# Retention attention and an ELU feed-forward on one core: half of the attention re-cut into chunks of 64 neighbouring tokens, with a new opening

## The chip, the cores and the metric

The kernel runs on one core of a Trainium2 chip. A core has TensorE (PE: matrix products; PEld is its loading of weights), VectorE (DVE), ScalarE (ACT), GpSimd (POOL) and SyncE (SP), which here only issues transfers; 16 DMA engines move data between the chip's main memory and the core's working memory SBUF. Matrix products land in PSUM, from which VectorE and ScalarE read. The metric is the device time of one execution in microseconds (us), lower is better, given as the median of several runs.

## What is computed

```
q, k, v: 8 batches x 8 heads x 576 tokens x 64, f32
scores = (q @ k^T) / 8
ret    = scores * gamma_h^(i-j) for i >= j, else 0      (gamma_h = 1 - 2^(-5-h))
x      = (ret @ v), heads side by side                  -> 4608 x 512
h      = x @ w_in                                       (512 x 2048)
g      = where(h > 0, h, exp(min(h, 0)) - 1)
out    = g @ w_out                                      (2048 x 512) -> 4608 x 512 f32
```

The decay gamma^(i-j) is split into a factor for the query row and one for the key row, so that both can be scaled ahead. Inside a chunk of tokens the masked scores are formed; what earlier chunks contribute goes through a running 64x64 sum of k^T v per head, the state.

## The kernel before

**Items.** A main item is one batch `b`, half `T` (tokens 0 to 255 or 256 to 511) and half `w` of the heads (four heads): 8 x 2 x 2 = 32 items, numbered 0 to 31 in batch order. The last 64 tokens of all batches make two tail items, four batches each. An item's tile of q, k or v has 128 partitions, and partition p holds the two neighbouring tokens 2p and 2p+1 of its 256 (`"h (p e) d -> p h (e d)"`, L375), so a piece read from main memory is 512 bytes. With `C = 64` partitions per chunk, a chunk is 128 tokens, two per item.

**Steps of an item.** Three loads on SyncE's queue (L375); q and k times their factors, four operations (L445, `cq`, `ck`), to bf16; v cast to bf16 (L479, `cv`); a transpose of q and k, for the first seven items on TensorE with copies back (L491, L497), from item 7 on by a DMA transpose on SyncE's queue (L530, `tr`). TensorE then makes scores (`do_scores`), state times queries (`do_inter`), values (`do_values`) and the new k^T v (`do_state`). VectorE multiplies the scores by the mask (L731, 1024 elements a partition). After the item's first chunk the running sum is `mid`, after its second `end` (L678 to L687); each is spread into a block-diagonal 128x128 tile, `s_mid` and `s_end` (L695, on GpSimd, or L709 for the first items). The result is copied into `xt` (L766), the input of the first layer.

**Stretches.** From the fifth item on, TensorE does one item's state times queries and values together with the next item's scores and k^T v, in one stretch (`stretch`). The first ones (`early`) come apart.

**Feed-forward.** Each block of 512 tokens (256 for the first three batches) goes through the first layer (`ffn1`: four matmuls, an exponential on ScalarE, then two VectorE operations, or one and one on ScalarE) and the second (`ffn2`), and out by SyncE. The weights come by GpSimd's queue in four pieces each (`wi0` to `wi3`, `wo0` to `wo3`).

**Order.** Nothing is ordered by hand: `Plan.run` plays the program through with a cost for each operation, transfers sharing the wire, a limit on buffers (`SLOTS`) and ranks, in which attention stands ahead of feed-forward by `LEAD`. What it picks is each engine's fixed program order. Constants named here: `HOP`, the time until another engine sees a result; `FROM`, when weight loads may be issued; `ON`, operations nailed to an engine; `AWAY`, a load put on ScalarE's queue (the first v). Where the plan leaves TensorE idle before 50 us, matmuls on zeros are put in.

Of the kernel before, what the change touches and what calls it, by code (L numbers as in the profile page):

```python
# [13 lines left out]
I32 = mybir.dt.int32  # L14
# [4 lines left out]
HOP = {"PE": 0.22, "DVE": 0.08, "ACT": 0.08, "POOL": 0.1}  # L19
# [3 lines left out]
class Op:  # L23


    def __init__(self, name, cost, deps, emit, rank, take=(), use=(), banks=(), dma=None, after=None):
        self.name, self.cost, self.emit, self.rank = name, cost, emit, rank
        self.deps = [d for d in deps if d is not None]
        self.turn = [] if after is None else [after]
        self.take, self.use, self.banks, self.dma = take, [*use, *(t[1] for t in take)], banks, dma  # L30
        self.eng = self.start = self.end = self.done = None
        self.slot, self.waits, self.at = {}, [], 0.0


class Plan:
# [6 lines left out]
    def add(self, *a, **kw):  # L42
        op = Op(*a, **kw)
        self.ops.append(op)
        for key in op.use:
            self.users.setdefault(key, []).append(op)
            op.turn += self.owner.get(key, [])
        for cls, key, *_ in op.take:
            self.owner[key] = [op]
            if cls not in FREE:  # L50
                op.turn += self.takers.get(cls, [])
                self.takers[cls] = [op]
        return op
# [12 lines left out]
    def run(self, began):  # L66

        self.left = {key: len(u) for key, u in self.users.items()}
        self.freed = {}
        bank, lanes = {}, {"SP": 0, "POOL": 0, "ACT": 0}  # L70
# [53 lines left out]
        while len(order) < len(self.ops) or any(wire.values()) or events:  # L124
            again = True
            while again:
                again = False
                for e in began:
# [9 lines left out]
                    op.eng, op.start, op.end = e, now, now + (cost[0] if isinstance(cost, tuple) else cost)  # L138
# [61 lines left out]
FROM = (8.9, 9.7, 10.5, 13.3, 16.6, 17.4, 18.2, 19.6)  # L200
ON = {}
DIRECT = True
AWAY = {("v", 0): 2.25}
# [7 lines left out]
FREE = ("f", "e", "em", "g", "ot")  # L211

# [4 lines left out]
    "xt": 3, "g": 28, "e": 4, "em": 4, "ot": 5, "mid": 4, "end": 4, "s_mid": 4, "s_end": 18,  # L217
# [4 lines left out]
def kernel(  # L222
# [56 lines left out]
    first = const.tile([P, 1], FP32, name="first")  # L279
    pin(nc.scalar.activation(first, zero[:, :1], AF.Exp))  # L280
# [13 lines left out]
    gk = const.tile([P, FT, H], FP32, name="gk")  # L294

# [58 lines left out]
    for n, it in enumerate(items):  # L354
        it.n = n
        it.early = n < FT
        it.xt = xt_of(it.blk)
        it.rank = n * 4 - 64 if it.early else base[it.blk] - LEAD + (
            16 * it.t if it.tail else 6 * it.w + (SPREAD * it.T if width[it.blk] > TB else 0))
# [3 lines left out]
    def load_main(it, srcs="qkv"):  # L363
# [3 lines left out]
        for s in srcs:  # L367
# [4 lines left out]

            def emit(op, src=src, key=key, away=away):
                dst = tiles[key].rearrange("p h e d -> p h (e d)")
                pin((nc.scalar if away else nc.sync).dma_start(  # L375
                    dst,
                    src[it.b, 4 * it.w : 4 * it.w + 4, 2 * P * it.T : 2 * P * (it.T + 1), :].rearrange(
                        "h (p e) d -> p h (e d)", e=2),
                ))

            take, use, held = [T(cls, key, [P, 4, 2, D], FP32)], [], []
            if s == "q" and n in HOLD:
                def emit_hold(op, key=key):
                    pin(nc.gpsimd.memset(tiles[key][:, 0, 0, :1], 0.0))

                held.append(add(f"hold{n}", {"POOL": 0.1}, [], emit_hold, -5, take=take))
                holds.append((held[0], HOLD[n]))
                take, use = [], [key]
            it.ld[s] = add(f"ld{s}{n}", {"ACT": 0.5} if away else {"SP": 0.46}, held, emit,
                           -10 ** 6 if away else len(plan.ops), take=take, use=use,  # L390
                           dma=(0.9, 32), after=None if away else chain.get(0))
# [28 lines left out]
    def load_w_in(n0, n1, after):  # L420
        c = slice(n0 * 512, n1 * 512)

        def emit(op):
            pin(nc.gpsimd.dma_start(w_in_sb[:, :, c], moe_w_in[:, c].rearrange("(j p) n -> p j n", p=P)))

        op = add(f"wi{n0}", {"POOL": 0.8}, [], emit, -1000, dma=(2.75 * (n1 - n0), 32 * (n1 - n0), 4.9), after=after)
        for n in range(n0, n1):
            w_in_ld[n] = op

    def load_w_out(n, after):  # L430
# [4 lines left out]
        w_out_ld[n] = add(f"wo{n}", {"POOL": 0.8}, [], emit, -1000, dma=(2.75, 32, 4.9), after=after)  # L435
# [3 lines left out]
    def scaled(it, i, e, cost):  # L439
        n = it.n  # L440
        key, raw = ("qkn", n), ("rq" + "qk"[i], n)
        g = (gq, gk)[i][:, 2 * it.T + e, 4 * it.w : 4 * it.w + 4].unsqueeze(2).to_broadcast([P, 4, D])
# [7 lines left out]
        op = add(f"c{'qk'[i]}{e}{n}", cost, [it.ld["qk"[i]]], emit, it.rank,  # L450
# [24 lines left out]
    def cast_v(it, cost):  # L475
        n = it.n

        def emit(op):
            pin(copy[op.eng](tiles["vn", n], tiles["rv", n]))  # L479

        it.cv = add(f"cv{n}", cost, [it.ld["v"]], emit, it.rank, take=[T("vn", ("vn", n), [P, 4, 2, D], BF16)],
                    use=[("rv", n)])

    def turn_pe(it, i, deps, src, key, dst_cls, n_of, cost):
# [8 lines left out]
        t = add(f"T{n_of}", {"PE": 0.35}, deps, emit, it.rank - 4,  # L493
# [12 lines left out]
    def prepare(it, turn):  # L506
# [21 lines left out]
        else:  # L528
            def emit(op):
# [3 lines left out]
                                 take=[T("qkT", ("qkT", n), [P, 8, P], BF16)], use=[("qkn", n)], dma=(1.7, 64)))  # L533
# [51 lines left out]

    def do_scores(it):
# [13 lines left out]
        tt = tiles["qkT", n]  # L600
        for hl in range(2):
# [9 lines left out]
    def do_inter(it, xkey):  # L611
        n = it.n
        if it.tail:
            for m in range(2):
                for j in range(2):
                    for hp in range(HP):
# [3 lines left out]
                            tiles["qkTt", n, m, j][:, hp, :ST])  # L620
            return
# [9 lines left out]
    def do_values(it, xkey):  # L631
# [12 lines left out]
        vn, pt = tiles["vn", n], tiles["pt", n]  # L644
        for hl in range(2):
# [7 lines left out]
    def do_state(it, views):  # L653
        n = it.n
        kn, vn = tiles["qkn", n], tiles["vn", n]
        for hl in range(2):
            for e in range(2):
                for c in range(2):
                    cs = slice(c * C, (c + 1) * C)
                    key, bank, ap = views[c]  # L660
                    for i in range(2):
                        acc(key, bank, i, ap()[i * D : (i + 1) * D, hl * D : (hl + 1) * D], kn[cs, 1, e, 2 * hl + i],
# [4 lines left out]
    def after_state(it, st, views, bank_keys):  # L667

        n = it.n
        prev = total.get(it.w) if it.T else None  # L670

# [48 lines left out]

    def mask_step(it, sc):
        n = it.n
        def emit(op):
            if it.tail:
# [5 lines left out]
                return  # L730
            pin(nc.vector.tensor_tensor(  # L731
# [5 lines left out]
        it.mask = add(f"mask{n}", {"DVE": 1.22}, [sc], emit, it.rank + 1,  # L737
                      take=[T("pt", ("pt", n), [P, 2, 2, 2 * P], BF16)], use=[("sc", n)], banks=[("sc", 0)])

    def inter_deps(it):  # L740
        if it.tail:
            return [*it.cvs, *(at[4 * it.t + j, 1, w].be for j in range(4) for w in range(2))]
        return [it.cv, it.bm] + ([at[it.b, 0, it.w].be] if it.T else [])

    def inter_uses(it):
# [3 lines left out]
        return [("s_mid", it.b, it.T, it.w), ("qkT", it.n), ("vn", it.n), ("pt", it.n)] + (  # L749
# [4 lines left out]
    def put_x(it, xkey, dep):  # L754

        for c in range(2):
            def emit(op, c=c):
# [4 lines left out]
                else:  # L762
                    src = xs[:, : 2 * P].rearrange("p (h e r) -> p h e r", h=2, e=2)
                    o = it.T * TB + c * P
                    dst = xt[:, 2 * it.w : 2 * it.w + 2, o : o + P].rearrange("p h (r e) -> p h e r", e=2)
                    pin(copy[op.eng](dst, src))  # L766
# [8 lines left out]
    def cost_of(it, parts):  # L775
        t = 0.0
        if "i" in parts:
# [18 lines left out]
    def stretch(prev, it):  # L796
# [12 lines left out]
        views = [((xkey, c), 0, lambda c=c: tiles[xkey, c][:, 2 * P : 3 * P]) for c in range(2)]  # L809
# [20 lines left out]
    def early(it):  # L830
        n = it.n
        sc = add(f"sc{n}", {"PE": 0.4}, it.turned, lambda op: do_scores(it), it.rank,
# [4 lines left out]
        st = add(f"st{n}", {"PE": 0.3}, [it.cq[1, 0], it.cq[1, 1], it.cv], lambda op: do_state(it, views), it.rank + 1,  # L837
# [112 lines left out]

    for it in items:
# [20 lines left out]
    def emit_factors(op):  # L972
        pin(nc.scalar.activation(gq[:, :FT], expo[:, :FT], AF.Exp, bias=bq))
        pin(nc.scalar.activation(gq[:, FT], expo[:, FT], AF.Exp, bias=bt))
        pin(nc.scalar.activation(gk, expo[:, :FT], AF.Exp, bias=bk, scale=-1.0))
# [36 lines left out]

    named = {op.name: op for op in plan.ops}
# [11 lines left out]
    order = plan.run({"PE": 1.3, "DVE": 2.2, "ACT": 2.25, "POOL": POOL0, "SP": 0.8})  # L1025
# [54 lines left out]
```

## Time and profile before

| | |
|---|---|
| median of 3 runs | 306.41 us (306.09 to 307.36) |
| the profiled execution | 306.02 us, of which the span shown is 303.8 us |
| busy: PE, DVE, ACT, POOL | 294.5, 210.1, 158.6, 148.3 us |
| granted TensorE clock | 1.0 throughout |
| main memory read, written | 36.70 MB, 9.44 MB |
| DMA packets under 512 B | 45841 of 103991 |

The span is the time from the first to the last instruction of the profiled execution. In a group's line stand: line of the program, engine, operation, tile written <- tiles read, size, count | busy time in us and mean ns of one | idle time of the engine before them, and what ended it. The row of 40 digits cuts the span into equal slices, each digit a busy share in tenths. The chain is the work that ended last, followed back from the end. Rows of the timeline give start, length, engine, line, operation and count. Rows of SPq, ACTq and POOLq are the issuing of transfers.

### The profile page before, as it was taken

To read this page: it belongs to the slowest core of one execution; us is meant where nothing else is said; L and a number is where in the kernel's file an instruction comes from. 1 tells how busy PE (TensorE), PEld (TensorE's weight loads), DVE (VectorE), ACT (ScalarE), POOL (GpSimd) and SP (SyncE) were. 2 spreads that over 40 slices of the span, in tenths; PEclk is the share of its full clock that TensorE was granted. 3 is DMA by queue.
4 is the path that set the end of the run, shared out by engine and by line. 5 is a ranking of instruction groups with operands and counts; after the bars stand their busy time and mean duration, and the time that the engine had idled before them with its cause. 6 is when DMAs were issued, how large, how long until landed. Compare 5 with 4: busy or idle time off the path is not lost.

```text
span 303.8 us, 8244 instructions
## 1 busy us (share of the span) xinstructions
PE 294.5 (97%) x3281; PEld 171.0 (56%) x3323; DVE 210.1 (69%) x380; ACT 158.6 (52%) x309; POOL 148.3 (49%) x252
## 2 busy tenths in 40 slices
PE   7899999999999999999999999999999999999996
PEld 3688656758767775554554444555554444444445
DVE  3978935749888888788787666768766666666600
ACT  4548724738765554687653434466544343444311
POOL 5980389987999998988886324322000000000000
PEclk9999999999999999999999999999999999999999
DMA  7999999999999999999997767311111111011132
GB/s 213 266 206 211 233 294 325 224 305 267 222 278 210 257 202 306 249 240 243 232 252 188 173 154 159 79 37 37 37 33 38 36 36 35 35 37 36 35 103 72
DMA packets 103991, 50.08 MB, mean 165 GB/s; under 512 B 45841, under 2 KB 99473, under 8 KB 103953
## 3 DMA queue, kind: packets, MB, share of 16 engines
q1 hardware_dynamic: 99200, 45.10, 67.4%
q0 software_dynamic: 4224, 4.19, 8.3%
q8 instruction: 26, 0.43, 0.6%
q10 hardware_dynamic: 528, 0.26, 0.3%
q14 instruction: 13, 0.10, 0.1%
HBM read 36.70 MB, written 9.44 MB: 152 GB/s over the span
## 4 chain that ended last, share of the span: by engine, by line
PE 92%; DVE 3%; DMA 2%; issue 1%; POOL 0%; SPq 0%; ACT 0%; POOLq 0%; ACTq 0%
PE f L256 88%; PE sc L256 4%; DMA rqk<-in_k_dram 2%; DVE qkn L445 1%; DVE pt L731 1%; PE f L491 1%; DVE g L900 0%; DVE f L890 0%; POOL qkn L445 0%; DVE qkT L497 0%; DVE s_mid L709 0%; SPq L375 0%; DVE xt L766 0%; DVE end L687 0%; DVE s_end L695 0%
## 5 line engine op out<-in xcount | busy, mean ns | idle before, releaser
L256 PE MATMUL f<-xt,w_in_sb 128*128 128x256 bf16 (+1 forms) x754 | 142.9, 325 | 1.0 <-DVE xt L766 0.3
L256 PE MATMUL f<-w_out_sb,g 128*128 128x512 bf16 (+2 forms) x580 | 139.8, 368 | 2.4 <-issue 1.3
L878 ACT ACTIVATE e<-f 128x512 f32<-128x512 f32 x144 | 85.6, 597 | 91.0 <-PE f L256 86.5
L256 PEld LDWEIGHTS <-w_in_sb 128*128 128x128 bf16 x768 | 73.3, 98 | 51.8 <-DVE xt L766 0.6
L256 PEld LDWEIGHTS <-g 128*128 128x128 bf16 x608 | 56.6, 98 | 58.9
L892 DVE TENSOR_SCALAR em<-e 128x512 bf16<-128x512 f32 x90 | 44.5, 494 | 44.3 <-ACT e L878 43.8
L902 DVE SCALAR_TENSOR_TENSOR g<-f,em 128x512 bf16<-128x512 f32 x90 | 61.9, 689 | 7.1 <-DVE em L892 0.5
L731 DVE TENSOR_TENSOR pt<-sc,mask 128x1024 bf16<-128x1024 f32 x32 | 38.9, 1215 | 5.3 <-PE sc L256 5.3
L445 POOL TENSOR_TENSOR qkn<-rqk,gq 128x256 bf16<-128x256 f32 x59 | 37.5, 648 | 10.2 <-DMA rqk<-in_q_dram 10.2
L900 DVE SCALAR_TENSOR_TENSOR g<-e,f 128x512 bf16<-128x512 f32 x54 | 36.4, 683 | 8.0 <-ACT f L888 7.6
L445 POOL TENSOR_TENSOR qkn<-rqk,gk 128x256 bf16<-128x256 f32 x62 | 38.6, 633 | 3.6 <-DMA rqk<-in_k_dram 3.6
L936 ACT COPY ot<-f 128x512 f32<-128x512 f32 (+2 forms) x36 | 20.2, 563 | 20.3 <-PE f L256 14.6
L766 ACT CAST xt<-f 128x256 bf16<-128x256 f32 x50 | 20.1, 450 | 18.6 <-PE f L256 18.5
L695 POOL TENSOR_TENSOR s_mid<-mid,diag 128x256 bf16<-128x256 f32 x29 | 17.8, 615 | 23.8 <-ACT mid L678 12.5
L888 ACT ACTIVATE f<-f 128x512 f32<-128x512 f32 x48 | 28.4, 595 | 0.0
L695 POOL TENSOR_TENSOR s_end<-end,diag 128x256 bf16<-128x256 f32 x31 | 19.6, 633 | 5.4 <-DVE end L687 5.3
L479 POOL CAST vn<-rv 128x512 bf16<-128x512 f32 x29 | 18.6, 643 | 2.4 <-DMA rv<-in_v_dram 2.4
L546 POOL TENSOR_TENSOR qkt<-rqt,gq 128x256 bf16<-128x256 f32 x16 | 10.5, 677 | 15.3 <-DMA rqt<-in_k_dram 15.3
L256 PE MATMUL sc<-qkT 64*64 64x128 bf16 x512 | 13.4, 222 | 0.0
L256 PE MATMUL f<-pt,vn 64*64 64x128 bf16 x512 | 12.7, 217 | 0.4 <-DVE pt L731 0.4
L256 PEld LDWEIGHTS <-qkT 64*64 64x64 bf16 x512 | 8.2, 106 | 4.0 <-DVE qkT L497 0.6
L687 DVE TENSOR_TENSOR end<-f,mid 128x128 f32<-128x128 f32 x32 | 9.0, 283 | 1.2 <-ACT mid L678 0.3
(69 smaller groups left out, 135.2 us busy)
## 6 DMA issues: line engine op xcount, KB each, us to landing
rqk<-in_q_dram SPq DMA_DIRECT2D x32, 256.0 KB, 5.3
rqk<-in_k_dram SPq DMA_DIRECT2D x32, 256.0 KB, 5.4
rv<-in_v_dram SPq DMA_DIRECT2D x31, 256.0 KB, 5.0
out_dram<-ot SPq DMA_DIRECT2D x26, 256.0 KB, 2.9
out_dram<-ot SPq DMA_DIRECT2D x19, 128.0 KB, 2.3
w_in_sb<-in_moe_w_in_dram POOLq DMA_DIRECT2D x4, 512.0 KB, 9.2
w_out_sb<-in_moe_w_out_dram POOLq DMA_DIRECT2D x4, 512.0 KB, 14.9
rqt<-in_q_dram SPq DMA_DIRECT2D x8, 128.0 KB, 3.2
```

Of the source, the lines that this page charges most:

```text
L256: pin(nc.tensor.matmul(*a, **kw))
L445: pin(alu[op.eng].tensor_tensor(tiles[key][:, i, e], tiles[raw][:, :, e], g, ALU.mult))
L479: pin(copy[op.eng](tiles["vn", n], tiles["rv", n]))
L695: pin(alu[op.eng].tensor_tensor(tiles[key].rearrange("p h (j d) -> p h j d", j=2), tiles[src].unsqueeze(2).to_broadcast([P, 2, 2, D]), dia ...
L731: pin(nc.vector.tensor_tensor(tiles["pt", n].rearrange("p i h n -> p (i h) n"), tiles["sc", n].rearrange("p i (h n) -> p (i h) n", h=2), m ...
L766: pin(copy[op.eng](dst, src))
L878: pin(nc.scalar.activation(tiles[ekey], tiles[hkey], AF.Exp))
L888: pin(nc.scalar.activation(ph, ph, AF.Relu))
L892: pin(alu[op.eng].tensor_scalar_add(em, e, -1.0))
L900: pin(nc.vector.scalar_tensor_tensor(g, e, -1.0, ph, ALU.add, ALU.min))
L902: pin(nc.vector.scalar_tensor_tensor(g, ph, 0.0, tiles["em", blk, p], ALU.max, ALU.min))
L936: pin(copy[op.eng](tiles[okey][:, :cols], tiles[pkey][:, :cols]))
```

## The change

**Far items.** Main items from number 8 on (`FAR = 8`, the third batch onwards; 24 of 32) are cut otherwise. A tile's half `e` now holds 128 neighbouring tokens, one per partition, so a load is two transfers of 128 KB whose pieces are 256 bytes. A chunk is 64 neighbouring tokens, four per item, numbered x = 0 to 3. Scores are 16 matmuls of 64 columns, values likewise (before 128 columns); state times queries is one matmul of 64 columns per chunk and head pair, 8 for T=1, 6 for T=0 (the first chunk has no state), before 4 and 2 of 128. The mask works on 512 elements, with the triangular `mask_t` of the tail. There are four running sums per item instead of two, each with its block-diagonal tile. They have their own factors `far_q`, `far_k`, made once during the opening. `mid` goes from 4 to 6 buffers, `s_mid` from 4 to 8.

**Plan.** Planned wire time of a far load is 0.64 per half, of its transpose 1.9 (before 0.9 per load and 1.7). `LAP` frees an engine a little before an operation's end, `HOP` is set anew, and `BESIDE` adds time to certain VectorE and GpSimd operations where both run them at once.

**Opening.** The first v goes on SyncE's queue between the first k and the second q. The small exponential `first` is gone. Weight loads may start at other times, some operations are nailed to engines, among them the first v's cast to VectorE. In the built program all four early items' scores stand ahead of the first first-layer matmul; before, one group of eight such matmuls stood ahead of the fourth.

```diff
-HOP = {"PE": 0.22, "DVE": 0.08, "ACT": 0.08, "POOL": 0.1}
+LAP = {"PE": 0.0, "DVE": 0.09, "ACT": 0.11, "POOL": 0.03, "SP": 0.0}
+HOP = {"PE": 0.2, "DVE": 0.135, "ACT": 0.155, "POOL": 0.1}
+BESIDE = {"DVE": ("POOL", 0.4), "POOL": ("DVE", 0.2)}
...
-FROM = (8.9, 9.7, 10.5, 13.3, 16.6, 17.4, 18.2, 19.6)
-ON = {}
+FROM = (8.96, 10.28, 13.13, 15.23, 17.0, 17.0, 17.44, 17.82)
+ON = {'mid1': 'DVE', 'be2': 'DVE', 'md_1_0': 'ACT', 'xc1_2': 'DVE', 'cv0': 'DVE', 'md_1_1': 'ACT', 'cq12': 'DVE'}
-AWAY = {("v", 0): 2.25}
+FAR = 8
+FAR_LD = 0.64
+FAR_TR = 1.9
+AWAY = {}
...
-    first = const.tile([P, 1], FP32, name="first")
-    pin(nc.scalar.activation(first, zero[:, :1], AF.Exp))
...
+            if it.far:
+                for e in range(2):
+                    def emit_far(op, src=src, key=key, e=e):
+                        i0 = 2 * P * it.T + e * P
+                        pin(nc.sync.dma_start(tiles[key][:, :, e], src[it.b, 4 * it.w : 4 * it.w + 4, i0 : i0 + P, :].rearrange(
+                            "h p d -> p h d")))
...
+        if it.far:
+            for x in range(4):
+                for i in range(2):
+                    r = slice(i * D, (i + 1) * D)
+                    for c in range(2):
+                        cs = slice(c * C, (c + 1) * C)
+                        mm(sc[cs, i, x * C : (x + 1) * C], tt[r, 4 + x, cs], tt[r, x, cs], start=True, stop=True)
+            return
...
+            for x in range(4):
+                c, e = x % 2, x // 2
+                if it.T + x == 0:
+                    continue
+                s = tiles[("s_mid", it.b, it.T, it.w, x) if x else ("s_end", it.b, 0, it.w)]
+                for hl in range(2):
+                    acc((xkey, c), 0, 2, tiles[xkey, c][:, hl * P + e * C : hl * P + (e + 1) * C], s[:, hl],
+                        tt[:, e * 2 + hl, c * C : (c + 1) * C])
...
+    def after_far(it, st, views, bank_keys, prev):
+        for x in range(4):
+            c, e = x % 2, x // 2
+            key = ("end", n) if x == 3 else ("mid", n, x)
...
+            blk = add(f"b{x}_{n}", {"POOL": 0.62, "DVE": (0.42, 1.5)}, [run], emit_b, it.rank + 3,
+                      take=[T(name, out, [P, 2, P], BF16)], use=[key])
...
-        it.mask = add(f"mask{n}", {"DVE": 1.22}, [sc], emit, it.rank + 1,
+        it.mask = add(f"mask{n}", {"DVE": 0.69 if it.far else 1.22}, [sc], emit, it.rank + 1,
```

More of the change, by code (lines that the diff above doesn't have):

```diff
@@ L137, in run @@
                     cost = op.cost[e]
[L138 removed]
+                    pay = cost[0] if isinstance(cost, tuple) else cost
+                    if op.side and e in BESIDE and now + 0.15 < busy.get(BESIDE[e][0], 0.0):
+                        pay += BESIDE[e][1]
+                    if op.side:
+                        busy[e] = now + pay
+                    op.eng, op.start, op.end = e, now, now + pay - (LAP[e] if op.dma is None else 0.0)
                     op.done = None
@@ L356 @@
         it.early = n < FT
+        it.far = n >= FAR and not it.tail
         it.xt = xt_of(it.blk)
```

126 lines of the change are left out of this document (106 added, 20 removed).

## The prediction

> **What bounds the kernel now.** I read the page first: busy shares, the 40 slices, the chain that ended last and the costliest groups.
>
> ```profile
> PE 294.5 (97%) x3281; PEld 171.0 (56%) x3323; DVE 210.1 (69%) x380; ACT 158.6 (52%) x309; POOL 148.3 (49%) x252
> DMA  7999999999999999999997767311111111011132
> PE 92%; DVE 3%; DMA 2%; issue 1%; POOL 0%; SPq 0%; ACT 0%; POOLq 0%; ACTq 0%
> L256 PE MATMUL f<-xt,w_in_sb 128*128 128x256 bf16 (+1 forms) x754 | 142.9, 325 | 1.0 <-DVE xt L766 0.3
> L256 PE MATMUL f<-w_out_sb,g 128*128 128x512 bf16 (+2 forms) x580 | 139.8, 368 | 2.4 <-issue 1.3
> L731 DVE TENSOR_TENSOR pt<-sc,mask 128x1024 bf16<-128x1024 f32 x32 | 38.9, 1215 | 5.3 <-PE sc L256 5.3
> L445 POOL TENSOR_TENSOR qkn<-rqk,gq 128x256 bf16<-128x256 f32 x59 | 37.5, 648 | 10.2 <-DMA rqk<-in_q_dram 10.2
> rqk<-in_k_dram SPq DMA_DIRECT2D x32, 256.0 KB, 5.4
> qkT<-qkn SPq DMA_TRANSPOSE x25, 4.9
> ```
>
> TensorE is the chain (92%) and the two feed-forward groups are almost all of it. The waits of TensorE from 24 us to the end, longest first, show that no other engine holds it up:
>
> ```profile
> PE f L256 <- issue: 1.3, 8, 0.2
> PE f L256 <- DVE xt L766: 0.3, 1, 0.3
> ```
>
> So every nanosecond of TensorE work taken out after about 24 us is a nanosecond off the span, as long as nothing else becomes late. The table by stages (busy time of PE, PEld, DVE, ACT and POOL with counts, then clock, DMA share, GB/s) shows what could:
>
> ```profile
> 60.00:100.00 40.00, 39.05 (x717) 28.90 (x723) 30.25 (x52) 24.48 (x52) 35.75 (x61) 1.00 1.19 250
> 100.00:155.00 55.00, 54.16 (x800) 31.48 (x802) 45.86 (x78) 35.33 (x73) 48.73 (x82) 1.00 1.23 253
> 155.00:195.00 40.00, 39.84 (x197) 18.23 (x202) 28.28 (x48) 17.93 (x31) 17.90 (x28) 1.00 0.77 167
> ```
>
> Until 155 us GpSimd (POOL) is busy 89% and the DMA engines are full; after it both have room. Attention runs ahead of the feed-forward work there, and that lead is the cover for anything the change makes slower.
>
> **Part 1: TensorE's attention stretches.** One stretch of today (its last 128x256 matmul is feed-forward again), and one tail stretch, which already works in chunks of 64; columns are start, length, line, operation, count:
>
> ```profile
> 99.11 0.28 PE L256 MATMUL f<-qkT,s_end 128*128 128x128 bf16 x2
> 99.22 0.28 PE L256 MATMUL f<-qkT,s_mid 128*128 128x128 bf16 x2
> 99.42 0.42 PE L256 MATMUL sc<-qkT 64*64 64x128 bf16 x16
> 99.67 0.39 PE L256 MATMUL f<-pt,vn 64*64 64x128 bf16 x16
> 99.89 0.29 PE L256 MATMUL f<-vn,qkn 64*64 64x64 bf16 x16
> 100.12 1.05 PE L256 MATMUL f<-xt,w_in_sb 128*128 128x256 bf16 x8
> ...
> 216.61 0.63 PE L256 MATMUL f<-qkTt,s_end 128*128 128x64 bf16 x16
> 217.17 0.45 PE L256 MATMUL sc<-qkTt 64*64 64x64 bf16 x32
> 217.44 0.44 PE L256 MATMUL f<-pt,vt 64*64 64x64 bf16 x32
> 217.81 0.39 PE L256 MATMUL f<-w_out_sb,g 128*128 128x512 bf16 x1
> ```
>
> By differences of starts: 16 score matmuls of 128 columns take 99.67 - 99.42 = 0.25 us, 16 value matmuls 0.22. The tail does 32 score matmuls of 64 columns in 217.44 - 217.17 = 0.27 us, so 16 in 0.135; the first group pays a little more, I take 0.15. Its 32 values take 0.37 with the change-over to 128 rows (about 0.12, as state at 99.89 shows against four groups of 0.031), so 16 in 0.125. Gain of a far item: 0.10 + 0.095 = 0.195 us.
>
> Against it stand more state-times-query matmuls. Before, an item has 2 (T=0) or 4 (T=1) of 128 columns; 99.11 to 99.22 is two, 0.055 each. After, 6 or 8 of 64 columns; the tail's 16 take 0.56 with a change-over of some 0.09 (99.11 to 99.42 less four of 0.055), so 0.029 each. T=0: 0.175 - 0.11 = +0.065; T=1: 0.235 - 0.22 = +0.015. Net 0.13 (T=0) and 0.18 us (T=1). Of the 32 main items 24 are far, 12 of each kind: 12 x 0.13 + 12 x 0.18 = **3.7 us less**. This is on the path. Ends: if the first groups cost more, 3.0; if the scores take the tail's bare 0.135, 4.1. The state matmuls stay 16 of 64x64, the feed-forward matmuls are the same in number and shape.
>
> **Part 2: what the far items cost elsewhere.** VectorE: the mask goes from 1024 to 512 elements, 1.215 us to about 0.69 (planned; half would be 0.61), and two more running sums at 0.28 come in: about even. GpSimd: seven operations per item become nine (four diagonal blocks in place of two), the engine doing 82 in 48.73 us, 0.594 each, so 4.2 to 5.35 us per item, in all 47 more, +28 us, of which none is on the path while attention keeps its lead. The factors for the far items (an iota, two VectorE operations, two exponentials, about 1 us) come in when those engines have gaps, or delay one g by that: 0 to 0.3 us.
>
> The lead is set by the order. On TensorE's queue there were 70.2 us of feed-forward matmuls (at 0.216 per 512 columns) between the scores of item 8 and item 27; now there are 99.7. Per item that is 70.2/19 = 3.7 plus a stretch of 0.95, 4.65 us, before; 5.25 plus 0.85, **6.1 us**, after. So GpSimd's 5.35 fits.
>
> SyncE and the DMA engines: three loads of 256 KB in 512-byte pieces become six of 128 KB in 256-byte pieces. Windows with only 512-byte loads, with only the tail's 256-byte loads, and with mostly a transpose:
>
> ```profile
> 94.20:96.80 2.60, 2.44 (x61) 1.88 (x57) 2.16 (x4) 1.53 (x4) 2.60 (x5) 1.00 1.21 293
> 173.00:173.75 0.75, 0.75 (x5) 0.34 (x4) 0.73 (x1) 0.00 (x0) 0.45 (x1) 1.00 1.15 243
> 97.40:99.60 2.20, 2.20 (x29) 1.53 (x31) 1.64 (x4) 0.99 (x2) 2.02 (x4) 1.00 1.31 91
> ```
>
> 256 KB at 293 GB/s is 0.895 us; 128 KB at 243 is 0.54, so 1.08 for what took 0.895, +0.185 x 3 per item. Today's pitch of 4.65 less 2.69 of loads leaves at most 1.95 for transposes and stores; with more stores in the longer pitch I take 2.1. After: 6 x 0.54 + 2.1 = 5.3 us of 6.1. Issuing on SyncE is tighter:
>
> ```profile
> 94.58 1.83 SPq L530 DMA_TRANSPOSE qkT<-qkn  x1
> 172.94 0.61 SPq L403 DMA_DIRECT2D rqt<-in_q_dram  x1
> 173.60 0.63 SPq L403 DMA_DIRECT2D rqt<-in_k_dram  x1
> 103.61 0.27 PE L256 MATMUL f<-qkT,s_mid 128*128 128x128 bf16 x2
> ```
>
> Six loads at 0.62, a transpose at 1.83 and a store at 0.5 are 6.05 us, just the pitch. The transpose issued at 94.58 is item 17's (the eleventh, item 7 being the first); with the median 4.9 us it lands at 99.5, and its stretch begins at 103.61: 4 us in hand. I cost this part at 0, covered by those 4 us; the other end is in the rivals.
>
> The order shows where it is tightest: the second tail item's scores stood after 167.3 us of feed-forward work, now after 184.6, behind 24 second-layer matmuls in a row.
>
> **Part 3: the opening.** The chain there:
>
> ```profile
> 1.32 4.73 DMA rqk<-in_k_dram
> 6.22 0.83 POOL qkn L445
> 7.42 0.42 DVE qkT L497
> 8.52 1.21 DVE pt L731
> ...
> 13.01 1.85 DVE qkn L445 x3
> 19.06 0.35 PE sc L256 x16
> 23.24 0.45 DVE xt L766
> ```
>
> ```profile
> 1.24 0.49 ACTq L375 DMA_DIRECT2D rv<-in_v_dram  x1
> ```
>
> The first k lands at 6.05, and beside it v runs on ScalarE's queue and takes its share of the engines. Moved behind k on SyncE's queue, v leaves k alone: 256 KB is 0.9 us of DMA time, so k lands 0 to 1.2 us earlier; I take 1.0. v then lands where k did, and its cast is now VectorE's (0.42), before the first mask. Every later load has the same bytes ahead of it: 0. The first-activation warm-up (0.2 us) goes; its table load stays in front of the factors: 0. VectorE has more to do from the first mask to the fourth: by the order and the rows (1.21 a mask, 0.41 copies, blocks and products, 0.28 sums, 0.45 xt copies) 11.2 us against 11.5, and three products that may meet GpSimd at 0.83 instead of 0.41 in place of three that did: even. Where that ends:
>
> ```profile
> 19.46 1.23 DVE L731 TENSOR_TENSOR pt<-sc,mask 128x1024 bf16<-128x1024 f32 x1 [0.20 <-PE sc L256]
> ```
>
> Before, feed-forward runs without a break from 23.24 + 0.45 = 23.7, when by the order 34 first-layer matmuls of 0.109 (3.7 us) were already done: as if it had begun at 20.0. After, the fourth mask begins at 19.46 - 1.0 = 18.5, ends at 19.7, values and change-overs take 0.65 to 20.35, and only 8 such matmuls (0.9 us) stand before them: as if begun at 19.45. So k's gain of 1.0 is worth about half of itself: **0.5 us less** taken, between 1.2 less and 1.5 more (k not earlier and VectorE's added xt copies and blocks, 0.45 and 0.41 each, on the path).
>
> **Sum.** The profiled execution took 306.02 us (span 303.8): less 3.7, less 0.5, plus 0.2 of small waits behind three block writes in place of one: 302.0. The median of the runs shown is 0.4 above the profiled execution, so **302.4 us**, 1.3% below 306.41.
>
> **Rivals.** *A 256-byte piece costs what a 512-byte one does.* Then a half load takes 0.895 us, an item 6 x 0.895 + 2.1 = 7.5 us of DMA against 6.1, over 20 items 28 us late less 4 in hand: +24, 326 us. It decides from 0.70 us per half on ((6.1 + 4/20 - 2.1)/6). The row against it is 243 GB/s at 173 us.
> The Trainium skill, "DMA: Bandwidth & Descriptors", Specifications, says that line rate needs pieces of at least 512 B and that smaller ones are read, modified and written; its section "Why small descriptors are slow" gives 27% for 256 B. By the first this rival is right; by the second, an estimate, a half load is about 0.57 us and nothing stalls; the trace's 243 against 293 GB/s (17% lower) sides with the second.
>
> *GpSimd becomes the bound, slower than before.* Nine operations of 0.594 fit; at 0.65, the mean of its rows counted one by one, 5.85 still fits. From 0.70 on the pitch breaks; at 0.75 (products beside VectorE took 0.83) an item takes 6.75, 20 items 13 us, less 4 in hand: TensorE waits 9 us, mostly at the tail item's scores, and the time is 302.4 + 9 = 311. For it: 89% busy today. Against it: 82 operations at 0.594 with VectorE beside them.
>
> *The opening eats it.* k no earlier and VectorE's additions on the path, +1.5 in place of -0.5, and some stalls: 304.4 to 306.
>
> *TensorE does not get shorter* because 64-column groups are bound by weight loads: the tail's rows exclude it, no time given.
>
> **Numbers.** Forecast (301 to 304): 0.66. Opening better than taken, below 301: 0.06. Opening eats it, 304 to 306.5: 0.13. GpSimd, 306.5 to 312: 0.10. 256-byte pieces: 0.05. The range is 300.8 to 306.6, leaving out the two last and a little of the second. A measurement here tells 0.5%, 1.5 us: faster (below 304.9) 0.77, same 0.11, slower 0.12.
>
> **What would show it.** Right: score rows of a far item about 0.14 us apart to the next group, eight state rows at 0.03; TensorE's waits still below 2 us after 24 us; a first k landing near 5 us; 256-byte loads above 210 GB/s; POOL about 177 us busy. Wrong: a wait of PE on `qkT` transposes or `s_mid` between 60 and 235 us, longest ahead of the tail scores; a first w_in matmul later than 19 us.

## The result and the profile after

| | before | after |
|---|---|---|
| median of all executions | 306.1 us (22) | 304.31 us (22) |
| lowest and highest | 305.45 and 307.91 us | 302.76 and 309.32 us |
| the profiled execution (span) | 306.02 us (303.8) | 305.64 us (303.9) |

The ratio is 0.9934, interval 0.9917 to 0.9951: faster by 0.66%, 2.0 us. Four of after's executions, at a lower granted clock (0.993 to 0.994), took 307.5 us or more; the ratios here and below leave such executions out, the medians count them. The forecast was 302.4 us: the direction is right, and half of the gain is missing. After's other 18 executions still lie over 3 us apart (302.76 to 306.49), and the profiled one is among the slowest of them; so the traces are compared stage by stage below.

The page of after: busy time of the engines, the DMA engines by slices, and the shares of the chain.

```profile
PE 291.6 (96%) x3378; PEld 169.6 (56%) x3418; DVE 214.2 (70%) x436; ACT 155.2 (51%) x305; POOL 178.4 (59%) x300
DMA  7999998999899999989999999987667101011132
PE 85%; DMA 6%; DVE 3%; issue 2%; SPq 1%; POOL 1%; ACT 1%; POOLq 0%; DVEq 0%; ACTq 0%
```

TensorE is 2.9 us shorter and GpSimd 30 us longer, both near the forecast, but TensorE's share of the chain fell from 92% to 85%, and DMA has 6% of it. TensorE's waits of after, first from 24 us to the end, then in the opening (14 to 24 us):

```profile
PE f L268 <- issue: 1.7, 11, 0.2
PE sc L268 <- DMA qkTt<-qkt: 1.7, 1, 1.7
PE f L268 <- DVE g L1020: 0.7, 1, 0.7
```

```profile
PE f L268 <- ACT vn L510: 0.9, 1, 0.9
PE f L523 <- DVE end L755: 0.5, 1, 0.5
```

Three of these are new and longer than 0.6 us: for a transpose of the tail, for an ELU result near 133 us, and for a cast of v at 17 us. The stretch itself did what was forecast; a far item with T=1, TensorE's timeline of after:

```profile
112.33 0.22 PE L268 MATMUL f<-qkT,s_end 128*128 128x64 bf16 x2
112.38 0.34 PE L268 MATMUL f<-qkT,s_mid 128*128 128x64 bf16 x6
112.65 0.32 PE L268 MATMUL sc<-qkT 64*64 64x64 bf16 x16
112.80 0.30 PE L268 MATMUL f<-pt,vn 64*64 64x64 bf16 x16
112.93 0.30 PE L268 MATMUL f<-vn,qkn 64*64 64x64 bf16 x16
113.16 1.04 PE L268 MATMUL f<-w_out_sb,g 128*128 128x512 bf16 x3
```

From the first state matmul to the next feed-forward matmul it is 0.83 us; before, from 99.11 to 100.12, 1.01: 0.18 less, as forecast for T=1. A stretch with T=0 takes 0.77 us (92.56 to 93.33) where it took 0.90 (103.61 to 104.51): 0.13 less, as forecast too.

**A balance by stages.** The order says how much feed-forward work stands ahead of an item's scores (0.216 us per 512 columns, 0.1095 per 256, 0.056 per 128; 249.5 in all). The time at which these scores start, less that work, is what all else has cost TensorE until then. For item 4 of before it is 37.20 - 16.61 = 20.59; item 4's scores are the first behind the opening, item 31's the last of a main item. These are the profiled executions, in us:

| kernel | until item 4 (opening) | item 4 to 31 | item 31 to the last matmul | sum |
|---|---|---|---|---|
| before | 20.59 | 27.06 | 3.66 | 51.31 |
| after | 21.06 | 24.55 | 5.33 | 50.94 |

The middle lost 2.5 us. The end took 1.7 us back, the opening 0.5.

**The end.** Chain of after ahead of the second tail item's scores, and TensorE there (start, length, what):

```profile
225.56 0.60 SPq L1062
...
226.21 0.66 SPq L432
...
226.91 3.41 DMA rqt<-in_k_dram
...
230.48 1.11 POOL qkt L578 x2
...
231.69 2.48 DMA qkTt<-qkt
...
234.21 0.31 PE sc L268 x15
```

A load of 3.4 us, two products of 1.1, a transpose of 2.5, one behind the other. `rqt` has two buffers, each for a pair of tail loads (q and k), so the plan can't place a pair until the products of the pair two before it are done. In this turn that buffer was free at 223.6 us (products at 222.46); what held the load is its place on SyncE's queue, behind transposes and two output stores (L1062). Before, the scores behind this chain stood at 217.17 us and nothing waited; now the order has 17 us more feed-forward work ahead of them, and still they come 1.7 us too early for the transpose.

**The opening.** The first k is indeed early, but the last early load is late. VectorE's rows (first product of k; first to fourth mask), then ScalarE's cast of item 3's v and the load that it waits for in the chain, all of after:

```profile
4.74 0.42 DVE L475 TENSOR_TENSOR qkn<-rqk,gk 128x256 bf16<-128x256 f32 x1 [0.39 <-DMA rqk<-in_k_dram]
7.29 1.23 DVE L843 TENSOR_TENSOR pt<-sc,mask 128x1024 bf16<-128x1024 f32 x1 [0.26 <-PE sc L268]
11.39 1.21 DVE L843 TENSOR_TENSOR pt<-sc,mask 128x1024 bf16<-128x1024 f32 x1
15.76 1.21 DVE L843 TENSOR_TENSOR pt<-sc,mask 128x1024 bf16<-128x1024 f32 x1
18.88 1.23 DVE L843 TENSOR_TENSOR pt<-sc,mask 128x1024 bf16<-128x1024 f32 x1
```

```profile
17.11 0.62 ACT L510 CAST vn<-rv 128x512 bf16<-128x512 f32 x1 [3.31 <-DMA rv<-in_v_dram]
```

```profile
9.19 7.90 DMA rv<-in_v_dram
```

k's product stands 1.4 us earlier than before (6.14), the first mask 1.2 earlier (8.52), the second 0.2 (11.60), the third not at all (15.71), the fourth 0.6 (19.46). v of item 3, the twelfth load, is cast at 17.11; before, at 14.84.

### The profile page after: what moved, and what is told of

It is laid out like the page before. It is cut to its first block, busy times and chain, and to the rows that moved or that the text cites. A ratio compares the mean times of both kernels' runs of the same rounds, so it can differ in the third digit from the quotient of the medians.

```text
span 303.9 us, 8654 instructions
## 1 busy us (share of the span) xinstructions
PE 291.6 (96%) x3378; PEld 169.6 (56%) x3418; DVE 214.2 (70%) x436; ACT 155.2 (51%) x305; POOL 178.4 (59%) x300
## 4 chain that ended last, share of the span: by engine, by line
PE 85%; DMA 6%; DVE 3%; issue 2%; SPq 1%; POOL 1%; ACT 1%; POOLq 0%; DVEq 0%; ACTq 0%
PE f L268 82%; PE sc L268 3%; DMA rv<-in_v_dram 3%; DMA rqk<-in_q_dram 2%; DMA rqt<-in_k_dram 1%; DVE em L1010 1%; DVE g L1020 1%; DMA qkTt<-qkt 1%; DVE g L1018 1%; SPq L404 1%; PE f L523 0%; ACT e L996 0%; POOL qkn L475 0%; POOL qkt L578 0%; DVE mid L803 0%
## 5 line engine op out<-in xcount | busy, mean ns | idle before, releaser
L1010 DVE TENSOR_SCALAR em<-e 128x512 bf16<-128x512 f32 x88 | 49.2, 560 | 35.3 <-ACT e L996 34.7
L812 POOL TENSOR_TENSOR s_mid<-mid,diag 128x256 bf16<-128x256 f32 x72 | 44.5, 630 | 15.1 <-DVE mid L803 9.5
L475 POOL TENSOR_TENSOR qkn<-rqk,far_q 128x256 bf16<-128x256 f32 x48 | 31.0, 658 | 1.8 <-DMA rqk<-in_q_dram 1.6
L475 POOL TENSOR_TENSOR qkn<-rqk,far_k 128x256 bf16<-128x256 f32 x48 | 31.0, 660 | 0.0
L837 DVE TENSOR_TENSOR pt<-sc,mask_t 128x512 bf16<-128x512 f32 x24 | 16.4, 681 | 5.9 <-PE sc L268 5.9
L803 DVE TENSOR_TENSOR mid<-f,mid 128x128 f32<-128x128 f32 x48 | 13.8, 288 | 3.5
L812 POOL TENSOR_TENSOR s_end<-end,diag 128x256 bf16<-128x256 f32 x24 | 15.6, 648 | 0.1
L475 POOL TENSOR_TENSOR qkn<-rqk,gq 128x256 bf16<-128x256 f32 x13 | 8.3, 648 | 12.0 <-DMA rqk<-in_q_dram 11.9
L843 DVE TENSOR_TENSOR pt<-sc,mask 128x1024 bf16<-128x1024 f32 x8 | 9.7, 1219 | 2.1 <-PE sc L268 2.0
L268 PE MATMUL sc<-qkT 64*64 64x64 bf16 (+1 forms) x512 | 11.0, 204 | 0.0
```

Of the source, the lines that this page charges most:

```text
L268: pin(nc.tensor.matmul(*a, **kw))
L475: pin(alu[op.eng].tensor_tensor(tiles[key][:, i, e], tiles[raw][:, :, e], g, ALU.mult))
L812: pin(alu[op.eng].tensor_tensor(tiles[out].rearrange("p h (j d) -> p h j d", j=2), tiles[key].unsqueeze(2).to_broadcast([P, 2, 2, D]), dia ...
L837: pin(nc.vector.tensor_tensor(far_pt(n).rearrange("p (i x) n -> p i x n", i=2), tiles["sc", n][:, :, : 4 * C].rearrange("p i (x n) -> p i ...
L1010: pin(alu[op.eng].tensor_scalar_add(em, e, -1.0))
```

## The experiments

The runs are called first, second and so on in the order in which they stand here. The balance of each profiled execution stands at the end of this section. Ratios are against before on the same chip.

**The far items with the opening of before.** `FROM`, `ON`, `AWAY`, `first`, `LAP`, `HOP` and `BESIDE` are put back.

```diff
-FROM = (8.96, 10.28, 13.13, 15.23, 17.0, 17.0, 17.44, 17.82)
-ON = {'mid1': 'DVE', ...}
-AWAY = {}
+FROM = (8.9, 9.7, 10.5, 13.3, 16.6, 17.4, 18.2, 19.6)
+ON = {}
+AWAY = {("v", 0): 2.25}
```

> The far items alone: the opening (first v on ScalarE's queue, weight release times, nailed operations, warm-up exponential) and the plan's engine times (LAP, HOP, BESIDE) as before the change. Theory: the shorter stretches are worth 3.7 us and stay; the new opening costs about 0.5 us, measured on the trace of after by the time at which the feed-forward work would have begun (20.55 against 20.0 us), and goes; what is lost late, a wait of VectorE near 132 us and the wait for the second tail item's transpose (1.7 us) may stay, since the tail scores stand at the same place in TensorE's queue (183.7 us of feed-forward work against 184.6). So 0.980 to 0.992 of before. Rival: the opening is worth its 0.5 us gain as predicted and only the late waits ate it; then this is 0.5 us slower than after, 0.995 or more.

304.43 us, ratio 0.9942 (0.992 to 0.9964): the far items alone give the whole measured gain.

**The new opening alone.** `FAR = 99`, so that no item is far.

> The opening and the plan's engine times alone, no far item (FAR beyond the last item; the far factors are still made). Theory: 0.3 to 0.9 us slower than before, 1.001 to 1.003, with the feed-forward work beginning as if at 20.4 to 20.6 us, because the third early item's v lands at about 17 us behind weights that were released sooner. Rival (my prediction): 0.5 us faster, 0.998, with that point at 19.5 us.

306.54 us, ratio 1.0007 (0.9989 to 1.0024): the opening and the plan's new times give nothing. In its balance the opening is 0.2 us shorter than before's, the stretch from item 4 to 31 1.0 us longer.

**Four buffers for the tail's loads.**

```diff
-    "rqt": 2, "rvt": 2, "qkt": 2, "vt": 4, "qkTt": 8,
+    "rqt": 4, "rvt": 4, "qkt": 2, "vt": 4, "qkTt": 8,
```

> After with four buffers in place of two for the tail's loads (rqt, rvt). Theory: the tail's wait is a loop of load (3.4 us to landing), two products (1.1) and transpose, kept serial by two buffers and by SyncE's order; with four the loads run ahead, the 1.7 us wait of TensorE before the second tail item's scores goes, and the time is 1 to 2 us below after, 0.986 to 0.990 of before. Rival: DMA bandwidth is short because of the 256-byte pieces, so that more buffers change nothing: within 0.5 us of after.

304.19 us, ratio 0.9917 (0.9891 to 0.9943). The wait on `qkTt` is gone and the end costs 3.39 us in place of 5.33, yet the median hardly moved. In its profiled execution the late v had grown; ScalarE's cast:

```profile
18.50 0.62 ACT L510 CAST vn<-rv 128x512 bf16<-128x512 f32 x1 [4.83 <-DMA rv<-in_v_dram]
```

So the tail was one of two losses, and the other differs from execution to execution. Whether it hid the gain in the median too is what the eighth run asks.

**Loads of 512-byte pieces.** A half load brings two heads of 256 tokens in place of four heads of 128.

```diff
-                        pin(nc.sync.dma_start(tiles[key][:, :, e], src[it.b, 4 * it.w : 4 * it.w + 4, i0 : i0 + P, :].rearrange(
-                            "h p d -> p h d")))
+                        pin(nc.sync.dma_start(
+                            tiles[key][:, 2 * e : 2 * e + 2].rearrange("p h e d -> p h (e d)"),
+                            src[it.b, 4 * it.w + 2 * e : 4 * it.w + 2 * e + 2, 2 * P * it.T : 2 * P * (it.T + 1), :].rearrange(
+                                "h (p e) d -> p h (e d)", e=2)))
```

> After, its order of compute kept, but each half load of a far item brings two heads in 512-byte pieces instead of four heads in 256-byte pieces: as many transfers and bytes, half the packets. Tokens stand in the old order, so the far items' part of the output is not the reference's. Theory: small pieces are covered, so within 0.7 us of after, with the tail's wait and the late v of the opening still there. Rival: the small pieces make the transfers late, then 1.5 us or more below after and no wait for the tail's transpose.

306.55 us, ratio 1.0004 (0.9982 to 1.0026), so larger pieces gain nothing. It is no clean price of a piece: a product now waits for both halves, and TensorE waits 0.5 us for `s_mid`.

**The first weight load behind one more product.** Four tail buffers, and `wi0` is issued behind item 2's first q product.

```diff
+    wi0 = named["wi0"]
+    order.remove(wi0)
+    order.insert(order.index(named["cq02"]) + 1, wi0)
```

> Four buffers for the tail's loads as in the third run, and the first weight load is issued behind item 2's first q product instead of ahead of it, some 0.6 us later. Theory A (the last early load of v finishes packet by packet beside the weights, so that TensorE gets it late in many executions): v's cast begins before 15.5 us, TensorE's wait for it is gone, the time is 302.5 to 303.3 and the runs lie closer together than 302.8 to 304.9. Theory B (the late v is chance and costs nothing on the whole, weights bind instead): the first w_in matmul waits for weights, 304.2 or more.

304.61 us, ratio 0.9926 (0.9899 to 0.9953). The weights' first packet came at 12.48 us, in the third run at 12.44, although the issue began 1.3 us later (10.72 against 9.38): issued this early, they start near the end of the eleventh load (12.3 and 12.5). In the two runs below that issue them later still, at 12.72 and 15.50, they start 1.6 us behind the issue. v's cast began at 15.79, TensorE's wait for it was gone, but a wait of 1.8 us for a later v (GpSimd's cast, between items 4 and 7) came in.

**A smaller last load.** Four tail buffers; item 3's v is a quarter.

```diff
+                if s == "v" and n == 3:
+                    pin(nc.sync.dma_start(dst[:, :1], src[it.b, 4 * it.w : 4 * it.w + 1, 2 * P * it.T : 2 * P * (it.T + 1), :].rearrange(
+                        "h (p e) d -> p h (e d)", e=2)))
+                    return
...
-            pin(copy[op.eng](tiles["vn", n], tiles["rv", n]))
+            src = tiles["rv", n][:, :1].to_broadcast([P, 4, 2, D]) if n == 3 else tiles["rv", n]
+            pin(copy[op.eng](tiles["vn", n], src))
```

> Four buffers for the tail's loads, and item 3's v is loaded for one of its four heads only (64 KB in place of 256 KB; its cast repeats that head, so the rows of item 3 are not the reference's). All else stands as in the third run. Theory A: the weights no longer catch the load, v's cast begins by 14 us in every execution, the time is 302.2 to 303.0 with runs inside 1 us. Theory B (the spread and the missing gain have another source): 303.9 to 304.4, spread as in the third run.

303.7 us, ratio 0.991 (0.9876 to 0.9944), runs still 4 us apart (302.0 to 306.1). TensorE's wait for v is gone, though the cast began at 14.99, and the weights now start at 11.71 and catch the loads of item 3's q and k as well; GpSimd's row:

```profile
14.03 0.85 POOL L479 TENSOR_TENSOR qkn<-rqk,gq 128x256 bf16<-128x256 f32 x1 [1.50 <-DMA rqk<-in_q_dram]
```

Theory A was too narrow: not this load is late, but whichever loads are unfinished when the weights start.

**VectorE's backlog at 132 us.** Four tail buffers, and two operations go to ScalarE.

```diff
-ON = {..., 'cq12': 'DVE'}
+ON = {..., 'cq12': 'DVE', 'oc_5_1_0': 'ACT', 'md_8_3': 'ACT'}
```

> Four buffers for the tail's loads, and two VectorE operations ahead of the wait near 132 us go to ScalarE (an output copy of block 5 and one ELU part of block 8). Theory C (VectorE's backlog there costs TensorE 0.7 to 0.9 us for good): TensorE's wait for g is gone and the time is 0.7 to 0.9 us below the third run's. Theory D (the backlog only moves to the next g, or the lost time is made up by a later cover): a wait for g or for ScalarE elsewhere, time within 0.3 us of the third run's 304.2.

302.73 us, ratio 0.9866 (0.9829 to 0.9902), the best of all. TensorE's waits after 24 us are these alone:

```profile
PE f L268 <- issue: 1.7, 11, 0.2
```

The middle costs 23.73 us in place of 24.55, which is the wait: theory C. By the built order only the output copy stands ahead of that wait; the ELU part of block 8 stands behind it, so it had no share in this except through the plan, which was made anew. The median fell by more than these 0.8 us; the profiled opening was 2 us better than the third run's (v waited for 0.7 us here, 2.3 there), and that part is the opening's chance, not the edit's.

**The opening of before with four tail buffers.** The kernel of the first run, and `"rqt": 4, "rvt": 4`.

> The far items with the opening and the plan's times of before (as in the first run, 304.4), and four buffers for the tail's loads. If the tail's wait of 1.4 us is on the path that sets the end: 302.9 to 303.2. If freeing the tail gains nothing because something else ends as late: 304.2 to 304.5. With the opening of before the weights begin with fewer packets of v left, so its runs should lie within 1.5 us.

303.46 us, ratio 0.9897 (0.9873 to 0.992), and all its runs lie within 0.6 us. Against the first run (0.9942) the tail's buffers are worth 0.45%, 1.4 us, here where no late v disturbs: the tail's wait was on the path. The two intervals just touch (0.992); together they leave 0.4 to 2.4 us, an estimate. DMA packets by queue between 14.4 and 17.4 us (queue: packets, MB, share; q0 are the weights, q1 the loads), of after, the third run and this one:

```profile
q0 software_dynamic: 609, 0.61, 121.6%
q1 hardware_dynamic: 24, 0.01, 1.9%
```

```profile
q0 software_dynamic: 589, 0.59, 117.5%
q1 hardware_dynamic: 80, 0.04, 6.2%
```

```profile
q0 software_dynamic: 620, 0.62, 124.3%
```

After the weights have started, what is left of a load is served beside them: 24 and 80 packets of 512 bytes are still under way at 14.4 us with the new opening, none in this run and 13 in the first, with the old one. The packet records show the last ones of the third run 0.11 us apart, one packet of the load (0.04 us) and then weights, up to 18.09 us. The Trainium skill, "DMA: Bandwidth & Descriptors", "Queues, rings and completion order", says that each DMA engine takes turns between the queues that it has work for, a whole packet of typically 9 to 17 descriptors at a time; the turns agree, but here they come record by record, 512 bytes each. That the twelve loads are all on SyncE's queue in the new opening goes with it: the eleventh ends at 12.1 to 12.5 us there, and at 11.9 to 12.1 where the first v runs on ScalarE's, a small difference.

**Weights later.** The seventh run's kernel; in one `wi0` and `wi1` stand behind item 2's k products, in the other `wi0` to `wi2` behind item 3's products.

```diff
+    for late, behind in (("wi0", "ck12"), ("wi1", "wi0")):
+        order.remove(named[late])
+        order.insert(order.index(named[behind]) + 1, named[late])
```

```diff
+    for late, behind in (("wi0", "cq13"), ("wi1", "ck03"), ("wi2", "ck13"), ("wi3", "wi2")):
```

> The kernel of the seventh run (four tail buffers, the wait near 132 us taken out; 302.7 us, v's cast 0.7 us late in its profile); only the first two weight loads are issued behind item 2's k products, some 1.5 us later. Theory A (the last v shares its DMA engines with the weights): the weights start at 12.9 us or later in place of 12.2, fewer than 300 packets of v are left then in place of 431, TensorE's wait for v goes, time 301.5 to 302.3, runs within 1 us. Theory B: weights start where the 11th load ends whatever their issue, as in the fifth run; nothing changes, 302.7.

> The kernel of the seventh run; the first weight load is issued behind item 3's first q product and each of the next two behind one of item 3's k products, so that all loads of the opening are done first (3 us later). Theory A: v's cast begins by 14.3 us in every execution and the first feed-forward matmuls stand 0.5 to 1 us earlier, 301.0 to 302.0, unless the weights now come last: then TensorE waits for w_in between 19 and 35 us, up to 1 us, 302.5 to 303.5. Theory B (late v is not a cost): 302.7 or above.

The first: ratio 0.9903 (0.988 to 0.9926), from four executions of 302.4 to 304.2 us. The weights start at 14.37, all twelve loads are done by 14.03, and v's cast begins at 14.55: theory A as far as the cause goes, but not in its time. The opening is no shorter than the seventh run's (20.81 against 20.43), and a new wait stands behind it; TensorE's waits after 24 us, and GpSimd's cast that it waits for:

```profile
PE f L268 <- issue: 1.7, 11, 0.2
PE f L268 <- POOL vn L510: 1.6, 1, 1.6
```

```profile
39.75 0.61 POOL L510 CAST vn<-rv 128x512 bf16<-128x512 f32 x1 [3.90 <-DMA rv<-in_v_dram]
```

The likely reason, not tested: the loads of items 4 to 7 now meet the weights later on. The second: 306.05 us, ratio 0.9977 (0.9954 to 1.0001); TensorE waits 0.9 us for `w_in_sb` and 1.4 for `w_out_sb`. From 9 to 40 us the DMA engines are full (busy share 0.98 up to 20 us and 1.2 behind it in the first of the two), and in both a transfer put back only moved the wait.

**The first v on ScalarE's queue.** The seventh run's kernel with the load back.

```diff
-AWAY = {}
+AWAY = {("v", 0): 2.25}
```

> The kernel of the seventh run, but the first v is loaded on ScalarE's queue as before the change (the opening is planned anew around it). Theory A (with all twelve loads on one queue the last ones end later and more of v is left when the weights start: 415 to 540 packets against 220 to 284 with v on ScalarE's queue): at most 300 packets are left, no wait for v, runs within 1 us, 302.0 to 302.6; the first k lands near 6 us again. Theory B (the first k 1 us earlier is worth 0.5 us or more): 303.0 to 303.8.

306.7 us, ratio 1.0012 (0.9994 to 1.003), its opening 3.9 us longer than the seventh's. Its load side went as theory A has it (143 packets left when the weights start, no wait for the last early v), but the plan came out anew and put more onto VectorE, whose masks stand at 9.22, 13.94, 17.43 and 21.36 us without a gap. So it doesn't price the early k alone, and what that is worth with everything else kept is open.

| kernel | opening | item 4 to 31 | end | sum |
|---|---|---|---|---|
| far items, opening of before | 21.60 | 23.88 | 5.01 | 50.49 |
| new opening alone | 20.39 | 28.03 | 3.66 | 52.08 |
| four tail buffers | 22.45 | 24.55 | 3.39 | 50.39 |
| 512-byte pieces | 20.51 | 25.44 | 4.50 | 50.45 |
| four buffers, first weights behind one product | 20.73 | 26.40 | 3.39 | 50.52 |
| four buffers, small last v | 20.73 | 24.55 | 3.40 | 48.68 |
| four buffers, no backlog | 20.43 | 23.73 | 3.39 | 47.55 |
| opening of before, four buffers | 22.00 | 23.88 | 3.39 | 49.27 |
| no backlog, weights behind k | 20.81 | 25.41 | 3.40 | 49.62 |
| no backlog, weights last | 23.62 | 25.32 | 3.40 | 52.34 |
| no backlog, first v on ScalarE's queue | 24.30 | 24.49 | 3.39 | 52.18 |

## Why the prediction was half right

**Part 1, TensorE's stretches: right.** 0.18 us of a T=1 item and 0.13 of a T=0 item were forecast and measured. Where nothing interferes (the seventh run) item 4 to the end costs 23.73 + 3.39 = 27.12 us against 30.72 before, 3.6 less; forecast were 3.7 less 0.2 of small waits.

**Part 2, loads and GpSimd: the rivals fell.** GpSimd was forecast at about 177 us and is 178.4, and does not stop TensorE. The 256-byte pieces are no bound: in the windows of after where nearly all bytes came in them, the rate (last column) is as high as the forecast asked for, and by the fourth run, as far as it goes, 512-byte ones gain nothing. The estimate of 0.57 us for a half load puts 27% on top of the time of a 512-byte piece; by the formula behind that figure (the Trainium skill, "DMA: Bandwidth & Descriptors", "Why small descriptors are slow": 3 cycles on the 8 that 256 bytes take) a 512-byte piece pays 3 on 16 as well, and a half load is about 0.52 us, an estimate. The sum did not go by it.

```profile
90.30:92.30 2.00, 2.00 (x15) 1.27 (x13) 1.24 (x2) 0.86 (x2) 2.00 (x4) 1.00 1.30 250
170.00:172.00 2.00, 2.00 (x11) 0.89 (x10) 1.78 (x4) 0.72 (x2) 2.00 (x5) 1.00 1.30 250
```

**Part 2, "4 us in hand … costed at 0": the step that failed, 1.4 us.** Those 4 us were read from a main item's transpose at 99 us. The text even named the second tail item's scores as the tightest place, and then gave that place the main item's cover. The tail's load, products and transpose follow one another through two buffers and one queue, and one pass adds up to 7 us; its own rows should have been laid end to end. The first against the eighth run prices it at 1.4 us in the median, the balance at 1.6 to 1.9 in the profiled executions.

**Part 2, "VectorE … about even": right for the far items, and 0.8 us wrong in one place of after.** VectorE is busy for 208.0 us in the first run (far items, plan's times of before) and for 216.3 in the second (no far item), against 210.1 before and 214.2 after: the rise of 4.1 us goes with the new plan, not with the far items. In after VectorE runs into a backlog near 132 us that makes TensorE wait once. The rows are VectorE's output copy and three of its ELU parts (`em`) ahead of that wait, and TensorE's first second-layer group of block 6, which waits.

```profile
125.68 0.68 DVE L1054 COPY ot<-f 128x512 f32<-128x512 f32 x1
...
127.95 1.54 DVE L1010 TENSOR_SCALAR em<-e 128x512 bf16<-128x512 f32 x2
...
131.21 0.73 DVE L1010 TENSOR_SCALAR em<-e 128x512 bf16<-128x512 f32 x1
```

```profile
133.73 2.53 PE L268 MATMUL f<-w_out_sb,g 128*128 128x512 bf16 x11 [0.70 <-DVE g L1020]
```

The seventh run took that wait away and 0.82 us of the middle with it. In the first run, TensorE waits for such a result for 0.2 us in all, and its middle costs 23.88 us, close to the seventh's; in the second there is no such wait. So it takes the far items and the new plan together. The mean over the kernel was even enough; the sum did not look at the one place where an output copy, a column of ELU parts and three running sums come together. The three `em` operations took 0.73 to 0.77 us each where 0.42 is their short time (last section), 1.0 us more together; no run tells this from the copy.

**Part 3, the opening: mechanism half right, size wrong.** k came 1.4 us earlier (1.0 forecast), but "every later load has the same bytes ahead of it: 0" was the wrong step. The bytes are the same; the queue is not, and what counts for the last loads is how much of them is left when the weights start. Where v does little harm the forecast of the fourth mask (18.5) holds: it stands at 18.35 in the second run and at 18.25 in the seventh, against 19.46 before. At its best the new opening is 0.1 to 0.2 us better than before's (20.39 to 20.51 against 20.59), not 0.5; where v comes late it was up to 0.5 (after) and 1.9 us worse (third run), and this differs between executions. The new opening alone measured 1.0007. Put into the far kernel, the opening of before cost 21.6 to 22.0, more than in its own kernel; its plan came out anew too (third mask at 16.91 us), so the two openings are not compared part for part.

**The sum.** Forecast: -3.7 - 0.5 + 0.2 = -4.0. Measured: -3.6 in the stretches with the small waits, +1.4 at the tail, +0.8 behind VectorE, which is -1.4, and for the opening between -0.2 and +1.9. The ratio says -2.0; the parts come from single executions of a kernel whose executions lie 3 us apart, and the 0.6 us between the two sums are not settled. One thing points to the tail: the fastest executions with two and with four buffers agree, 302.76 (after) and 302.81 (third run), 303.16 (first) and 303.12 (eighth). So the tail's wait, too, may cost little in some executions, though both profiled ones show it; after's one trace is of a long execution (305.64 us), so this stays open. Two of the signs listed as wrong came true, the wait ahead of the tail scores and a first first-layer matmul later than 19 us (TensorE of after):

```profile
19.50 1.05 PE L268 MATMUL f<-xt,w_in_sb 128*128 128x256 bf16 x8
```

Both waits after 24 us are gone in the seventh run's kernel, whose 302.73 us is near the 302.4 forecast, and faster than both kernels shown.

## What to carry to other kernels

Slack read at one stage holds for that stage only: ahead of the tightest place, lay its own rows (load, product, transpose) end to end, and count the buffers that close the loop. When TensorE work is taken out between fixed covers, every chain that was just in time needs its own sum, and a mean that is "even" says nothing of the one place where several operations meet. In an opening where transfers fill the DMA engines, an earlier first load can be lost again at the last one; look at which transfers are unfinished when a large stream starts beside them.

## What was not expected of the hardware

VectorE's `em` operations (SBUF to SBUF) became slower; groups of before and of after, mean ns in the column before the last:

```profile
L892 DVE TENSOR_SCALAR em<-e 128x512 bf16<-128x512 f32 x90 | 44.5, 494 | 44.3 <-ACT e L878 43.8
```

```profile
L1010 DVE TENSOR_SCALAR em<-e 128x512 bf16<-128x512 f32 x88 | 49.2, 560 | 35.3 <-ACT e L996 34.7
```

One by one they take either about 0.42 us (a few up to 0.50) or over 0.5 us, and every long one has a GpSimd operation beside it: 22 of 90 before, 41 of 88 after, while none of the 54 and 30 without one is long. Of the short ones 14 and 17 have a GpSimd operation beside them too. A busier GpSimd alone does not do it: in the first run it is busy for 176.6 us (148.3 before, 178.4 after), and 26 of 86 are long, the mean 501 ns; it depends on which operations meet. The `g` operations, which read PSUM and one SBUF tile, stayed at 689 ns. The Trainium skill, "SBUF — State Buffer", "Who interferes with whom", has this as a port pair that VectorE shares with GpSimd, taken for a whole instruction in a mode that `tensor_scalar` can enter; the counts of both kernels agree with it. The cost, 88 x 66 ns = 5.8 us of VectorE, is more than the whole rise of its busy time.

Some of ScalarE's `xt` casts went the other way, 450 to 390 ns in the mean. They are the far items': 390 also in the first run, 450 in the second, which has no far item. A far item writes neighbouring columns of `xt`, another item every second one; that this is the cause is not shown.
